# A gated attention and convolution kernel: the loading of x, the score bound and the share of VectorE in the exponentials are changed

## The chip, the cores and the metric

The kernel runs on one core of a Trainium2 chip. The core has a matrix engine (TensorE, PE in the profile), a vector engine (VectorE, DVE), an activation engine (ScalarE, ACT), a general engine (GpSimd, POOL) and a queue engine (SyncE, SP), all of which run at the same time and wait for each other through semaphores. The metric is the device time of one execution in microseconds (us), the median of several runs. TensorE writes to PSUM, a memory of eight banks of 128 x 512 float32; everything else lies in SBUF, which has 128 partitions.

## What is computed

Two branches are computed from the same x (2048 tokens x 640 features, bf16) and mixed by a gate, one number for each token. The first is a long convolution; the second is attention with 32 heads of size 20 that share one key and one value head.

```python
def reference(A_q, A_k, A_v, A_shift_k, A_ssm_k, A_ssm_D, B_x, B_wq, B_wk, B_wv, B_wo, gate_w):
    def _A_ref(q, k, v, shift_k, ssm_k, ssm_D):       # a convolution, by FFT
        ...                                           # k shifted by 4 taps, kv = k_shift * v
        y = y + kv * ssm_D[None, None, :]
        return q * y
    def _B_ref(x, wq, wk, wv, wo):
        H, Dh = 32, 20
        q = (x @ wq).reshape(B, S, H, Dh) ...
        k = x @ wk                                    # one key head for all 32 query heads
        v = x @ wv
        scores = jnp.einsum("bhqd,bkd->bhqk", q, k) * (Dh ** -0.5)
        p = _softmax(scores, axis=-1)
        o = jnp.einsum("bhqk,bkd->bhqd", p, v)
        return o ... @ wo
    x = A_q
    g = _sigmoid((x * gate_w).sum(-1, keepdims=True))
    return g * _A_ref(x, ...) + (1 - g) * _B_ref(x, ...)
```

The softmax needs 32 x 2048 x 2048 exponentials. The kernel doesn't subtract the true maximum of a row from the scores but an upper bound of it, the length of the query times the length of the longest key, in front of a fixed offset of 256 (`UP`).

## The kernel before

A small scheduler in Python, with an estimate of the duration of each operation, fixes at build time the order of the instructions on each engine. On the chip each engine then works through its list strictly in that order: an instruction that waits holds back all that stand behind it. A smaller `prio` goes first among what the scheduler thinks is ready.

**The stream of exponentials.** There are 32 groups G (four query blocks of 512 tokens x eight groups of four heads). Each has 16 key chunks j and four heads r, so there are 32 x 16 x 4 = 2048 score tiles of 128 keys x 512 queries. ScalarE takes them in turns of three tiles (`ETA`) and two tiles (`ETB`). `DVE_J[G]` lists the chunks j of a group from which two of the four tiles (a pair) go to VectorE instead.

```python
DVE_J = [()] * 5 + [(3, 8, 13)] * 27          # 27 groups x 3 = 81 pairs
...
def EXP(n):                                   # ScalarE, lines 1091
    op("act", lambda e: e.activation(et(n)[:, 0:w], self.ps[:, lo:lo + w], ACT.Exp, scale=SCALE), ...)

def DEXP(G, j):                               # VectorE: one pair, five instructions
    for h, r in enumerate(rs):                # two tiles, from PSUM to dW (line 1120)
        ... e.tensor_scalar(W[:, 512 * h:512 * h + 512], self.bank(bk), SCALE * LOG2E * 128.0, ...)
    V(lambda e: e.scalar_tensor_tensor(X[:, :], w, DP, w, ALU.add, ALU.mult), ...)            # 1123
    V(lambda e: e.scalar_tensor_tensor(X[:, :], X[:, :], DQ, w, ALU.add, ALU.mult), ...)      # 1124
    V(lambda e: e.scalar_tensor_tensor(T["ETd"]..., X[:, :], DA, W[:, :], ALU.mult, ALU.add)) # 1126
```

The products of a pair with the values come last in their group (`late_pv`): if VectorE is late with a pair, TensorE, and then ScalarE, waits at the end of the group.

**The prologue.** x is needed transposed (`xT`, features on partitions), in four blocks of 512 tokens. Three blocks come through transposing DMAs on SP's queue, the last one (block 3) is loaded plainly into `xn` and transposed by TensorE.

```python
def loads(self):
    ...                                       # wk, wv, gate_w, then 200 KB of wq on ScalarE's queue
    self.dma(T["wqst"][:, :, 0:160], wq[:, :, 0:160], ..., eng="act", prio=-98.6)
    self.dma(T["xn"][:, 12:16, :], x[:, 12:16, :], writes=[("xn", 3)], nbytes=655360, prio=-9)
    for b in range(NB - 1):                   # NB = 4
        xl = self.g.add("sp", lambda e, o=o, i=i: e.dma_start_transpose(o, i), (), [("xT", b)], 0.1, kind="d",
                        nbytes=655360, prio=-8 + b, lat=1.6)          # line 755
        xl.iss = 3.3
    ...
def tables(self):     # four rounds: VectorE makes the arguments, ScalarE the sine and the cosine
    ...               # and at last an Exp of one element, which draws in the table of Exp (line 831)
def kproj(self):
    for b in range(NB):                       # keys, replicated for four heads: group "kT", line 926
        ...
        self.evac(gr, "dve", None, ["mcol"], [("kT4", b)], ...)       # + mcol: -1 in row 20
    for b in range(NB):                       # keys, values, gate of each token: group "kvn", line 940
        ...
        self.evac(gr, "act", ... e.activation(T["ksq"]..., view(bk, 0), ACT.Square) ...)
        ...                                   # vaug, gsum; ksum: sum of the squares
    ...     # kmcol: maximum per partition; a matmul spreads it; kmaxr: maximum; kroot: its root; kmaxr: scaled
def qproj(self, I, gs, prio, banks, ng):      # queries: group "qp", line 982
    ...     # qT from PSUM; sq = qT * qT; matmul with IndG sums the squares of each head (line 998)
    self.evac(gr, "dve", ... ci[0:n, :], self.bank(bk)..., 0.5, float(0x1FBD1DF5), ALU.mult, ALU.add ...)   # root
    self.dve(lambda e: e.tensor_scalar(cr[0:n, :], ci[0:n, :].bitcast(F32), T["kmaxr"][0:n, 0:1], -UP,
                                       ALU.mult, ALU.add), [..., "kmaxr"], ["cr"], ...)                     # bound
    o = self.dma(qt[20:128:32, gs[0]:gs[0] + ng, :], cr[0:n, :], ..., name="crow")    # into row 20 of each head
    if I == 0 and gs[0] == 0:
        self.crow0 = [o]                      # much other work of the start is held back until this one
```

A score tile is then one matmul of `kT4` with `qT` over 32 rows: 20 of the head, and row 20, which subtracts the bound.

## Time and profile before

The time is 893.52 us, the median of 3 runs (893.17 to 894.32). The profiled execution has a span of 891.6 us.

| engine | busy us | share of the span | instructions |
|---|---|---|---|
| ScalarE | 868.3 | 97% | 779 |
| TensorE, matmuls | 855.1 | 96% | 7801 |
| VectorE | 658.2 | 74% | 867 |
| GpSimd | 365.6 | 41% | 311 |

The busy times count each instruction from its start to its end, and neighbours on one engine overlap a little, so the sum of the durations of a group of instructions can be above its share of the span. TensorE's list contains matmuls on zeros (916 of them at line 1511), which are only there to keep it going where it has nothing to do. The lines of the profile on which the prediction rests are shown there.

### The profile page before, as it was taken

To read this page: it belongs to the slowest core of one execution; us is meant where nothing else is said; L and a number is where in the kernel's file an instruction comes from. 1 tells how busy PE (TensorE), PEld (TensorE's weight loads), DVE (VectorE), ACT (ScalarE), POOL (GpSimd) and SP (SyncE) were. 2 spreads that over 40 slices of the span, in tenths; PEclk is the share of its full clock that TensorE was granted. 3 is DMA by queue.
4 is the path that set the end of the run, shared out by engine and by line. 5 is a ranking of instruction groups with operands and counts; after the bars stand their busy time and mean duration, and the time that the engine had idled before them with its cause. 6 is when DMAs were issued, how large, how long until landed. Compare 5 with 4: busy or idle time off the path is not lost.

```text
span 891.6 us, 17952 instructions
## 1 busy us (share of the span) xinstructions
PE 855.1 (96%) x7801; PEld 348.9 (39%) x7825; DVE 658.2 (74%) x867; ACT 868.3 (97%) x779; POOL 365.6 (41%) x311
## 2 busy tenths in 40 slices
PE   7899999999999999999999999999999999999997
PEld 3334434433433344433333334443444443343233
DVE  6457653298778788877879877768887678878674
ACT  5899999999999999999999999999999999999995
POOL 2950057860333377244427324268512677300000
PEclk9999999999999999999999999999999999999999
DMA  7930200010000011000001010000000000300211
GB/s 158 210 128 11 67 20 15 19 31 19 21 13 20 12 28 31 20 20 14 18 10 42 20 48 23 19 9 19 19 20 19 14 14 2 101 22 29 65 43 53
DMA packets 58371, 32.62 MB, mean 37 GB/s; under 512 B 41139, under 2 KB 54324, under 8 KB 58292
## 3 DMA queue, kind: packets, MB, share of 16 engines
q1 hardware_dynamic: 56026, 30.89, 12.5%
q8 instruction: 61, 1.00, 0.5%
q10 hardware_dynamic: 2266, 0.59, 0.3%
q14 instruction: 18, 0.15, 0.1%
HBM read 17.85 MB, written 6.02 MB: 27 GB/s over the span
## 4 chain that ended last, share of the span: by engine, by line
ACT 79%; PE 17%; DMA 2%; SPq 1%; DVE 1%; issue 0%; DVEq 0%
ACT ETA L1091 47%; ACT ETB L1091 32%; PE ps L1368 5%; PE ps L1059 5%; PE ps L1131 3%; PE ps L1310 1%; PE ps L982 1%; DMA kTr<-in_A_k_dram 1%; DMA xT<-in_A_q_dram 1%; SPq L755 1%; PE ps L1434 0%; SPq L1293 0%; PE ps L1511 0%; PE ps L1249 0%; DVE ETd L1126 0%
## 5 line engine op out<-in xcount | busy, mean ns | idle before, releaser
L1091 ACT ACTIVATE ETA<-ps 128x1536 bf16<-128x1536 f32 x378 | 593.4, 1570 | 3.9 <-PE ps L1059 3.4
L1091 ACT ACTIVATE ETB<-ps 128x1024 bf16<-128x1024 f32 x377 | 433.9, 1151 | 0.1
L1401 POOL TENSOR_TENSOR Pp<-X,K 128x512 f32<-128x512 bf16 x120 | 180.2, 1528 | 373.7 <-DVE K L1389 373.6
L1059 PE MATMUL ps<-qT,kT 32*128 32x512 bf16 x2048 | 300.2, 385 | 20.4 <-ACT ETA L1091 13.1
L1059 PEld LDWEIGHTS ps<-qT,kT 32*128 32x128 bf16 x2048 | 73.8, 91 | 255.4 <-ACT ETB L1091 121.7
L1131 PE MATMUL ps<-ETA,vaug 128*32 128x512 bf16 x1132 | 152.7, 385 | 0.0
L1120 DVE TENSOR_SCALAR dW<-ps 128x512 f32<-128x512 f32 x162 | 111.3, 687 | 50.7 <-PE ps L1059 49.4
L1131 PE MATMUL ps<-ETB,vaug 128*32 128x512 bf16 x754 | 148.5, 385 | 0.1
L1126 DVE SCALAR_TENSOR_TENSOR ETd<-dX,dW 128x1024 int16<-128x1024 f32 x81 | 110.6, 1366 | 25.3 <-PE ps L1131 25.0
L1123 DVE SCALAR_TENSOR_TENSOR dX<-dW 128x1024 f32<-128x1024 uint16 x81 | 111.7, 1380 | 0.9
L1124 DVE SCALAR_TENSOR_TENSOR dX<-dX,dW 128x1024 f32<-128x1024 f32 x81 | 108.7, 1341 | 0.5
L1401 POOL TENSOR_TENSOR AB<-Pp 128x256 bf16<-128x256 f32 x80 | 82.1, 1026 | 6.0
L1434 PE MATMUL ps<-AB,Tcos 128*128 128x256 bf16 x320 | 77.3, 275 | 0.0
L1511 PE MATMUL ps<-Tcos,zeros 128*32 128x512 bf16 x916 | 75.8, 385 | 0.3
L1434 PE MATMUL ps<-AB,Tsin 128*128 128x256 bf16 x280 | 68.6, 274 | 0.0
L1401 POOL TENSOR_TENSOR Pp<-Pp 128x512 f32<-128x512 f32 x40 | 61.0, 1524 | 3.1
L1368 PE MATMUL ps<-ssm_kT,Tcos 128*128 128x256 bf16 x320 | 55.3, 276 | 0.0
L1368 PE MATMUL ps<-kv,Tcos 128*128 128x256 bf16 x320 | 50.2, 275 | 0.1
L1368 PE MATMUL ps<-ssm_kT,Tsin 128*128 128x256 bf16 x320 | 49.1, 274 | 0.0
L1368 PE MATMUL ps<-kv,Tsin 128*128 128x256 bf16 x320 | 48.4, 274 | 0.0
L1131 PEld LDWEIGHTS ps<-ETA,vaug 128*32 128x32 bf16 x1132 | 29.3, 94 | 34.9 <-issue 34.0
L982 PE MATMUL ps<-xT,wq_pad 128*128 128x512 bf16 x137 | 38.9, 382 | 2.5 <-issue 1.3
(137 smaller groups left out, 746.8 us busy)
## 6 DMA issues: line engine op xcount, KB each, us to landing
rbc<-scr_d SPq DMA_DIRECT2D x31, 256.0 KB
scr_o<-oTn SPq DMA_DIRECT2D x24, 128.0 KB, 1.7
xn<-in_A_q_dram SPq DMA_DIRECT2D x4, 640.0 KB
kv<-in_A_v_dram SPq DMA_DIRECT2D x4, 640.0 KB, 4.8
out_dram<-outsb SPq DMA_DIRECT2D x14, 160.0 KB, 1.8
oTp<-scr_o SPq DMA_DIRECT2D x12, 160.0 KB, 2.8
wog<-in_B_wo_dram SPq DMA_DIRECT2D x4, 200.0 KB
wo<-in_B_wo_dram SPq DMA_DIRECT2D x4, 200.0 KB
```

Source lines behind the costliest of these rows:

```text
L982: o = self.mm(gr, lambda e, bk, gi=gi, dc=dc: e.matmul(self.bank(bk), T["wq_pad"][:, dc, 128 * gi:128 * gi + 128], T["xT"][:, dc, 512 * I: ...
L1059: return e.matmul(self.bank(bk), T["kT4"][32 * r:32 * r + 32, 128 * j:128 * j + 128], T[f"qT{G // 8 % 2}"][32 * r:32 * r + 32, G % 8, :], ...
L1091: op("act", lambda e: e.activation(et(n)[:, 0:w], self.ps[:, lo:lo + w], ACT.Exp, scale=SCALE), [("ps", base[n % 2] + k) for k in range(le ...
L1120: self.evac(gr, "dve", lambda e, bk, h=h: e.tensor_scalar(W[:, 512 * h:512 * h + 512], self.bank(bk), SCALE * LOG2E * 128.0, 128.0 * (127 ...
L1123: V(lambda e: e.scalar_tensor_tensor(X[:, :], w, DP, w, ALU.add, ALU.mult), [kW], ["dX"], c_ps(1024), **k)
L1124: V(lambda e: e.scalar_tensor_tensor(X[:, :], X[:, :], DQ, w, ALU.add, ALU.mult), [kW], ["dX"], c_ps(1024), **k)
L1126: V(lambda e: e.scalar_tensor_tensor(T["ETd"][:, :].bitcast(dt.int16), X[:, :], DA, W[:, :], ALU.mult, ALU.add), [kW, "dX"], ["ETd"], c_ps ...
L1131: return op("pe", lambda e: e.matmul(self.bank(6)[32 * r:32 * r + 32, :], T[va][:, j, :], src, start=(j == 0), stop=(j == NSC - 1), tile_p ...
L1368: self.mm(gr, lambda e, bk, lhs=lhs, rhs=rhs, comp=comp, n=n: e.matmul(self.bank(bk, 256, 256 * comp), lhs, rhs, start=(n == 0), stop=(n = ...
L1401: f = lambda e: e.tensor_tensor(out, a, b, alu)
L1434: self.mm(gr, lambda e, bk, lhs=lhs, fc=fc, comp=comp, h=h: e.matmul(self.bank(bk, 256, 256 * h), lhs, AB[:, fc, :, comp, :], start=(fc == ...
L1511: sch.filler = [[lambda e, r=r, st=st: e.matmul(self.bank(6)[32 * r:32 * r + 32, :], self.T["zeros"][:, 0:32], self.T["Tcos"][:, 0, 0:512] ...
```

## The change

The change does two things.

It hands more score tiles to VectorE: `DVE_J` names 89 pairs instead of 81. Groups 2, 3 and 4, which had none, get one each; five later groups get four instead of three; in many others the chunks move.

And it rebuilds the prologue. Half of x (blocks 2 and 3) is loaded plainly and transposed by TensorE, so that only two transposing DMAs are left; the second plain load goes out on ScalarE's queue, in the place of the first part of wq, which moves to the head of SP's queue. The bound is split: the length of the query stands in row 20 of the query and meets the length of the longest key (negative) in row 20 of the key; the offset 256 stands in row 21 of the query (`qup`) and meets a one in row 21 of the key (`q21`). So the row of the query no longer waits for the keys, and it is written in one instruction, the root as the upper 16 bits of a float, where it took two. The keys now wait for the maximum instead: `mcol` is made from it. The products "kvn" go ahead of the queries and keys, and the squares of the keys now have to come ahead of the loading of the table of Exp. Tables and constants that are not needed for the first scores get a later place.

```diff
-DVE_J = [()] * 5 + [(3, 8, 13)] * 27
+DVE_J = [(), (), (4,), (6,), (5,), (4, 9, 11), (3, 8, 13), (3, 8, 13), (3, 8, 13), (3, 9, 13), (3, 8, 13), (3, 8, 13), (2, 7, 12), (2, 6, 12), (3, 8, 14), (1, 6, 11), (3, 8, 13), (1, 8, 13), (1, 8, 12), (1, 6, 11), (1, 5, 9, 13), (3, 8, 13), (1, 4, 8, 14), (1, 6, 11), (3, 8, 12), (4, 7, 12), (2, 6, 10, 14), (2, 6, 10, 14), (1, 6, 11), (2, 6, 10, 12), (2, 9, 12), (3, 8, 13)]
 ... loads
-        self.dma(T["wqst"][:, :, 0:160], wq[:, :, 0:160], writes=[("wqst", 0)], nbytes=204800, eng="act", prio=-98.6)
+        self.dma(T["wqst"][:, :, 0:160], wq[:, :, 0:160], writes=[("wqst", 0)], nbytes=204800, prio=-10, lat=3.8)
-        self.dma(T["xn"][:, 12:16, :], x[:, 12:16, :], writes=[("xn", 3)], nbytes=655360, prio=-9)
-        for b in range(NB - 1):
+        self.dma(T["xn"][:, 12:16, :], x[:, 12:16, :], writes=[("xn", 3)], nbytes=655360, prio=-9, lat=3.8)
+        self.dma(T["xn"][:, 8:12, :], x[:, 8:12, :], writes=[("xn", 2)], nbytes=655360, eng="act", prio=-98.65, lat=3.8)
+        for b in range(NB - 2):
 ...
-                            nbytes=655360, prio=-8 + b, lat=1.6)
-            xl.iss = 3.3
+                            nbytes=655360, prio=-8 + b, lat=3.3)
+            xl.iss = 3.8
 ... tables
-            p, pr = c % 2, -2000.0 + c
+            p, pr = c % 2, (-2000.0 if c < 2 else -900.0) + c
 ... xT
-        b = NB - 1
-        for d0, nd in ((0, 2), (2, 2), (4, 1)):
+        for b, d0, nd in ((b, d0, nd) for b in (NB - 1, NB - 2) for d0, nd in ((0, 2), (2, 2), (4, 1))):
 ... kproj
-            gr = self.group("kT", (1.16 if b == 0 else 4.0) + 0.1 * b, banks=ALLB if b == 0 else (7, 4, 5))
+            gr = self.group("kT", (1.9 if b == 0 else 4.0) + 0.1 * b, banks=ALLB if b == 0 else (7, 4, 5))
-            gr = self.group("kvn", 1.5 + 0.1 * b, banks=ALLB)
+            gr = self.group("kvn", 0.9 + 0.01 * b, banks=ALLB)
 ...
+            self.sins[-1].deps.add(q)         # q: the squares; sins[-1]: the first Exp, with its table
 ...
-        self.dve(lambda e: e.tensor_scalar(T["kmaxr"][0:32, :], T["kroot"][0:32, :].bitcast(F32),
-                                           1.045 * 1.045 * 1.015, None, ALU.mult), ["kroot"], ["kmaxr"], ...)
+        self.dve(lambda e: e.scalar_tensor_tensor(T["mcol"][:, :], T["kroot"][:, :].bitcast(F32), T["m20"][:, 0:1],
+                                                  T["q21"][:, :], ALU.mult, ALU.add), ["kroot", "m20", "q21"],
+                 ["mcol"], 0.2, prio=-5000, name="kmax")
 ... qproj
-            self.evac(gr, "dve", None, (), [("qT", par, gi)], 0.7,
-                      alts=self.copy_alts(qt[:, gi, :], lambda bk: self.bank(bk)))
+            self.evac(gr, "dve", None, ["qup"], [("qT", par, gi)], 0.7, alts={...})     # + qup
 ...
-            ci[0:n, :], self.bank(bk)[0:n, :].bitcast(I32), 0.5, float(0x1FBD1DF5), ALU.mult, ALU.add), (), ...
-        self.dve(lambda e: e.tensor_scalar(cr[0:n, :], ci[0:n, :].bitcast(F32), T["kmaxr"][0:n, 0:1], -UP,
-                                           ALU.mult, ALU.add), ["ci", ("sq", 0), ("sq", 1), "kmaxr"], ["cr"], ...)
+            cr[0:n, :].bitcast(dt.int16), self.bank(bk)[0:n, :].bitcast(I32), 0.5 / 65536.0,
+            float(0x1FBD1DF5) / 65536.0, ALU.mult, ALU.add), (), ["cr"], c_ps(512), prio=pr)
 ... build
-            self.qproj(0, [2 * b, 2 * b + 1], 1.15 if b == 0 else 9.0 + 6 * b, ALLB if b == 0 else (7,), 2)
+            self.qproj(0, [2 * b, 2 * b + 1], 0.95 if b == 0 else 9.0 + 6 * b, ALLB if b == 0 else (7,), 2)
```

## The prediction

> **What bounds it now.** I read the page first for the share of each engine, then ScalarE's waits, then the chain of the first 24 us, ScalarE in the last microseconds, and the prologue on VectorE. The page:
>
> ```profile
> PE 855.1 (96%) x7801; PEld 348.9 (39%) x7825; DVE 658.2 (74%) x867; ACT 868.3 (97%) x779; POOL 365.6 (41%) x311
> ...
> ACT 79%; PE 17%; DMA 2%; SPq 1%; DVE 1%; issue 0%; DVEq 0%
> ```
>
> ScalarE and TensorE both look full, but 79% of the chain that ended last is ScalarE. All the waits of ScalarE after 24 us are one line:
>
> ```profile
> ACT ETA L1091 <- PE ps L1059: 3.4, 3, 2.3
> ```
>
> Three waits, 3.4 us together, all before 40.6 us. From there to the last exponential the stream never stops. Its ends, from the timeline:
>
> ```profile
> 40.56 1.45 ACT L1091 ACTIVATE ETA<-ps 128x1536 bf16<-128x1536 f32 x1 [0.31 <-PE ps L1059]
> ...
> 881.28 0.78 ACT L1091 ACTIVATE ETA<-ps 128x512 bf16<-128x512 f32 x1
> ```
>
> So the kernel has three parts: a prologue up to the first exponential at 23.98 us, a stream bound by ScalarE, and a tail from 882.07 us (end of the last one in the chain) to 891.6 us. The price of a tile: by the timeline six ETA and six ETB, 30 tiles, start before 40.56, and ScalarE does 2048 - 2 x 81 = 1886 in all. 1856 tiles in 841.5 us, less 0.3 for one small gate instruction, are 0.453 us each.
>
> The prologue, in the chain in order of time:
>
> ```profile
> 1.25 4.87 SPq L755
> 6.12 0.05 issue
> 6.17 6.21 DMA xT<-in_A_q_dram
> 12.38 0.04 issue
> 12.43 0.68 PE ps L940 x20
> 13.10 0.06 issue
> 13.16 2.10 PE ps L982 x9
> 15.26 1.08 PE ps L926 x5
> 16.34 0.22 PE ps L940 x9
> 16.56 0.67 ACT kT L933
> 17.23 0.02 issue
> 17.25 1.28 ACT L831
> ...
> 20.94 0.45 DVE cr L1007
> 21.39 0.03 DVE IndG L797
> 21.42 1.84 DMA qT<-cr
> ```
>
> Read three things in it. TensorE stands until 12.4 us in front of the second transposing DMA, although the first had come (the "kvn" of its block ran at 9.80); the third landed at 14.8, where SP went on. The table of Exp (L831, 1.28 us) stands in front of the last squares of the keys. And the row of the query (`cr`, then 1.84 us of DMA) waits for the maximum of the keys.
>
> [...] the trace has the 1.28 us, but the next instruction follows at once (18.54)[...]. [...] between 6 and 9 us the DMA share is already above 1, at 265 GB/s, so the second plain load will take its time from the transposes beside it. [...] `ci` from PSUM takes 0.67 us in the prologue, `cr` from SBUF 0.47, so the one instruction that is left costs what the first of the two cost. [...] the three long steps of a pair have a median of 1.22 us but means of 1.34 to 1.38 and a longest of 2.17[...].
>
> **Part 1, eight more pairs.** 2 x 8 = 16 tiles leave ScalarE: 16 x 0.453 = 7.25 us, all of it on the path, since the stream has no holes. VectorE gets 8 x (2 x 0.687 + 1.380 + 1.341 + 1.366) = 8 x 5.46 = 43.7 us, and loses about 4 us of `cr` (six at 0.67), so it is busy for some 698 us, 79% of the shorter span. On average that fits beside the stream. Locally: a group with four pairs has 64 - 8 = 56 tiles on ScalarE, 25.4 us, and in these VectorE has 4 x 5.46 = 21.8 us of pairs and about 1.8 us of normalization (0.69 + 0.25 + 0.90), before any work of the convolution. Between 570 and 810 us, where the five such groups (20, 22, 26, 27, 29) lie, VectorE was busy for 186.5 of 240 us already. Pairs have priority over the convolution, so the backlog falls on work that has time; but lists are fixed, and where one is late the end of a group stops ScalarE. Groups 2 to 4 lie at about 85 to 172 us, where VectorE is half idle (33.1 of 71 us from 100 to 171). For both I put down 0.8 us of new waits.
>
> **Part 2, the prologue.** The load: before, 1.97 MB of transposes and some 0.96 MB plain; after, 1.31 and 1.6 MB: the same 2.9 MB. The trace shows plain loads at about 358 GB/s (3.1 to 4.6 us) and transposes alone at about 290 (6.5 to 8.6). That is 1.31/0.29 + 1.6/0.358 = 9.0 us against 9.5, so the bytes alone bring little: the last block of x should land at about 13.2 us instead of 14.8. The gain lies in what follows.
>
> Path A, keys: landing 13.2; 20 small matmuls 0.68; squares 0.3; their sum 0.3; maximum per partition 0.2; spreading matmul 0.25; maximum 0.3; root and `mcol` 0.3; keys from PSUM 0.7; first scores 0.5. Together 3.5 us, so 16.7. The step from `kmcol` to scaled maximum took 19.79 to 20.88 before, which is the same size. Path B, query row: first transposed block at about 10 (behind two plain loads now), two queries 2.1 (13.16 to 15.26 before), copy 0.7, squares 0.4, matmul 0.6, root 0.67, DMA 1.84, scores 0.5: 16.8. Path C, the table: behind the last squares (14.2), 1.28 + 0.2, so 15.7: just hidden. Path D is plain work. ScalarE, from 4.4 us (its first table has come by then): eight sines and cosines at 0.62, half of six copies of transposed x (1.0, 1.0, 0.6 for each of two blocks, 2.6), a query 0.6, squares 1.0, table 1.5, keys 0.7: 11.4, so 15.8 without a hole. VectorE: 16 table steps of together 8.6, copies of x 2.0, indicators and columns 2, squares and maxima 1.9, queries and root 2.2: 16.7 from 0.8, so 17.5. TensorE does 40 transposes at 0.1 from 6.8 and about 6 us of products, so it is free enough.
>
> Four paths thus end between 15.8 and 17.5, and lists in fixed order never interlock without a hole; I take 0.5 us over the longest, 18.0 us. That is 6.0 us less than 23.98. What comes after the row of the query (loads of k and v, the rest of wq, tables) is tied to it and moves with it, so I leave the wait of 2.3 us at 37.7, for the transposed k, as it is. But the keys of blocks 1 to 3, done so far while ScalarE waited, now fall into the start of the stream: 0.1 to 0.3 us.
>
> **Sum.** 893.5 - 7.25 - 6.0 + 0.8 + 0.2 = 881.2 us.
>
> **Rivals.** (1) VectorE becomes the bound in the groups with four pairs and the new waits eat the first part. For it: 23.6 of 25.4 us there. Against it: the pairs don't have to follow the chunks in time (scores of any chunk are at hand), neighbours with three pairs leave room, and VectorE waited 49 us for scores of pairs and 25 us at `ETd`, which is slack. It would make 886 to 889. (2) The prologue gains little, because the two plain loads push the first transposing DMA back and VectorE's 17 us of work take the place of the DMA wait. For it: path D. Against it: the tables of the later rounds are out of the way of the squares now. First exponential at 20.5, total 883.7. (3) Everything overlaps and the wait for transposed k gets shorter too, since k starts to load before the stream does: first exponential at 16.5 and 2 us of the wait gone: 877.5. (4) The tail grows because the delayed work of the convolution reaches past the last exponential. VectorE was busy for 49.6 of 70 us from 810 to 880, so I give this little; it would cost 1 to 2 us.
>
> **Range and chances.** The first part is nearly fixed; its waits can spread over 0 to 4 us. The prologue can spread from -7.5 to -3.5. I say 877.5 to 886.0 for 8 in 10. Faster by 2% would need less than 875.6, which both parts at their best hardly reach: 0.03. Slower by 2% would need a stream that stops in many groups: 0.01. Within 2%: 0.96.
>
> **What would show it.** ScalarE's ETA and ETB together do 1870 tiles, with means near 1.57 and 1.15 us; the chain gives 2.26 us for each pair of them. The first ETA starts between 16.3 and 20.5 us. ScalarE's waits after its first exponential sum up to less than 6 us; VectorE is busy for about 698 us. In the chain of the prologue no table load stands in front of a square, and `cr` goes out without waiting for the keys. I am wrong if waits at the ends of groups (scores or products with VectorE's tiles) add up to over 5 us, or if the first exponential starts after 21 us, or if the tail is longer than 10.5 us.

## The result and the profile after

The changed kernel takes 886.86 us, the median of 4 runs (885.91 to 887.47), against 893.92 us of the kernel before, taken beside it. The ratio is 0.9918 with a 95% interval of 0.9901 to 0.9935. That is 7 us gained where the prediction had 12, and 0.9 us above the end of its range.

The page of the changed kernel: busy time of each engine, and the shares in the chain that ended last.

```profile
PE 851.3 (96%) x7736; PEld 347.1 (39%) x7736; DVE 685.2 (77%) x901; ACT 862.2 (97%) x773; POOL 377.3 (43%) x311
...
ACT 83%; PE 12%; DMA 2%; SPq 1%; DVE 1%; issue 0%; DVEq 0%
```

The kernel is still bound by ScalarE's stream. What the stream waits for, by the list of waits (total us, times, longest):

```profile
ACT ETA L1105 <- PE ps L1073: 5.1, 6, 2.5
```

The stream itself, from the timeline of ScalarE (start, duration, and in brackets the wait ahead of it):

```profile
23.24 1.45 ACT L1105 ACTIVATE ETA<-ps 128x1536 bf16<-128x1536 f32 x1
...
37.11 1.45 ACT L1105 ACTIVATE ETA<-ps 128x1536 bf16<-128x1536 f32 x1 [2.46 <-PE ps L1073]
...
41.21 1.45 ACT L1105 ACTIVATE ETA<-ps 128x1536 bf16<-128x1536 f32 x1 [1.49 <-PE ps L1073]
...
43.95 1.45 ACT L1105 ACTIVATE ETA<-ps 128x1536 bf16<-128x1536 f32 x1 [0.32 <-PE ps L1073]
...
235.92 1.45 ACT L1105 ACTIVATE ETA<-ps 128x1536 bf16<-128x1536 f32 x1 [0.50 <-PE ps L1073]
...
874.97 1.25 ACT L1105 ACTIVATE ETB<-ps 128x1024 bf16<-128x1024 f32 x1
```

Two things are to be seen. The first exponential comes at 23.24 us, only 0.7 earlier than before. And the start of the stream has two holes, 2.46 and 1.49 us, where it had one of 2.3. After 44 us ScalarE waits only three times, 0.16, 0.17 and 0.50 us, the last at 235.92 us; the kernel before had no wait there.

For all runs the span can be split in the same way: the first exponential, the score tiles on ScalarE at 0.4527 us each, what the stream takes beyond that, and the tail behind the last exponential. The price of a tile is that of `k_as_it_lands` below, whose stream has no wait at all: 847.51 us for 1872 tiles. (So the rest of that kernel is nought by the way it is counted; that it has no wait is measured.)

| kernel | first exponential | tiles | tiles x 0.4527 | rest of the stream | tail | span |
|---|---|---|---|---|---|---|
| before | 23.98 | 1886 | 853.8 | 4.3 | 9.5 | 891.6 |
| predicted | 18.0 | 1870 | 846.6 | 5.3 | 9.5 | 879.3 |
| changed | 23.24 | 1870 | 846.6 | 6.4 | 9.4 | 885.6 |

(The row "predicted" is the prediction's own sum: 858.1 us of stream before, less 7.25, plus 0.8 and 0.2.) The eight pairs have brought what they should. Of the 6.3 us between the two last rows, 5.2 lie ahead of the first exponential and 1.1 in the rest of the stream.

These are places in the span, though, and not yet causes. The eighth ETA, ahead of which 35 tiles are done in both kernels, starts at 43.95 us in the changed kernel. In the kernel before:

```profile
42.83 1.45 ACT L1091 ACTIVATE ETA<-ps 128x1536 bf16<-128x1536 f32 x1
```

The 0.7 us gained at the first exponential have become a loss of 1.1. What lies between is seen in the chain that ended last. In the changed kernel:

```profile
16.73 1.86 DMA qT<-cr
...
27.98 7.52 DMA kTr<-in_A_k_dram
```

and in the kernel before, behind its `21.42 1.84 DMA qT<-cr`:

```profile
27.70 7.96 DMA kTr<-in_A_k_dram
```

In both kernels this chain runs from the row of the query over the loads of the transposed k to TensorE and the next exponential, and not over the first exponential. The row went out 4.7 us earlier (16.73 instead of 21.42). But TensorE's list now waits there for the third block of k, where it waited for the second, and the two landed at nearly the same time, 35.50 and 35.66 us. So a first exponential at 18.0 us would have met this wait too. If the row had landed 2.3 us earlier, as predicted, the block would have come at some 33.2 us and the sixth ETA, which starts 1.6 us after it, at some 34.8; this is an estimate from the times above. The prediction had the sixth ETA at 37.71 - 6.0 = 31.7 us.

Why does the first exponential come so late? The first transposed block of x has landed at 10.87 us, in the chain:

```profile
1.80 9.07 DMA xT<-in_A_q_dram
```

The second transposed block of x had landed at 13.05 us (SP goes on at 13.07), as predicted (13.2). The row of the query no longer waits for the keys, also as predicted. But from 10.9 us on TensorE runs almost without a pause, 12.01 us of the 12.33 up to the first exponential. What it does with the time, from its timeline:

```profile
13.59 1.28 PE L905 MATMUL ps<-ident,xn 128*128 128x128 bf16 x20
...
15.33 1.18 PE L941 MATMUL ps<-wkv,xT 128*128 128x41 bf16 x40
16.35 1.24 PE L933 MATMUL ps<-xT,wk 128*128 128x512 bf16 x5
17.43 0.67 PE L941 MATMUL ps<-wkv,xT 128*128 128x41 bf16 x20
...
18.64 1.25 PE L992 MATMUL ps<-xT,wq_pad 128*128 128x512 bf16 x5
19.73 0.22 PE L961 MATMUL ps<-ident,kmcol 128*128 128x128 bf16 x1
```

The last "kvn" (L941, 17.43) is the start of the prediction's path of the keys. It begins 4.4 us after its block has landed, behind the transposes of the plainly loaded block 2 (whose data came at 10.3, but which stand behind the queries in the list), other "kvn", and keys. Then `kmcol` is done at 19.0, but the small matmul that spreads it (L961) has to wait for a query of block 1 (L992, 18.64), which nothing needs yet. That query is also copied by VectorE ahead of the maximum. And then the offset of the keys:

```profile
21.10 0.87 DVE L972 SCALAR_TENSOR_TENSOR mcol<-kroot,m,q 128x1 f32<-128x1 f32 x1
21.11 0.85 POOL L894 COPY wq_pad<-wqst 128x800 bf16<-128x800 bf16 x1
```

One number per partition takes 0.87 us, as long as the copy that GpSimd makes beside it (`offset_one_input` below tests this). From the landing to the first exponential it is 10.2 us; the prediction's path A had 3.5 and its half microsecond of holes.

### The profile page after: what moved, and what is told of

Its sections match the earlier page's. It is cut to its first block, busy times and chain, and to the rows that moved or that the text cites. A ratio compares the mean times of both kernels' runs of the same rounds, so it can differ in the third digit from the quotient of the medians.

```text
span 885.6 us, 17829 instructions
## 1 busy us (share of the span) xinstructions
PE 851.3 (96%) x7736; PEld 347.1 (39%) x7736; DVE 685.2 (77%) x901; ACT 862.2 (97%) x773; POOL 377.3 (43%) x311
## 4 chain that ended last, share of the span: by engine, by line
ACT 83%; PE 12%; DMA 2%; SPq 1%; DVE 1%; issue 0%; DVEq 0%
ACT ETA L1105 50%; ACT ETB L1105 34%; PE ps L1382 5%; PE ps L1073 3%; PE ps L1145 2%; DMA xT<-in_A_q_dram 1%; SPq L1307 1%; DMA kTr<-in_A_k_dram 1%; PE ps L992 1%; PE ps L1324 0%; SPq L597 0%; PE ps L1263 0%; DVE ETd L1140 0%; PE ps L1014 0%; PE ps L1386 0%; DVE dX L1137 0%
## 5 line engine op out<-in xcount | busy, mean ns | idle before, releaser
L1073 PE MATMUL ps<-qT,kT 32*128 32x512 bf16 x2048 | 297.5, 385 | 22.5 <-ACT ETA L1105 13.0
L1073 PEld LDWEIGHTS ps<-qT,kT 32*128 32x128 bf16 x2048 | 73.5, 91 | 259.3 <-ACT ETB L1105 121.7
L1134 DVE TENSOR_SCALAR dW<-ps 128x512 f32<-128x512 f32 x178 | 122.3, 687 | 47.2 <-PE ps L1073 45.5
L1140 DVE SCALAR_TENSOR_TENSOR ETd<-dX,dW 128x1024 int16<-128x1024 f32 x89 | 123.7, 1389 | 24.1 <-PE ps L1145 23.7
L1137 DVE SCALAR_TENSOR_TENSOR dX<-dW 128x1024 f32<-128x1024 uint16 x89 | 118.9, 1336 | 0.4
L1138 DVE SCALAR_TENSOR_TENSOR dX<-dX,dW 128x1024 f32<-128x1024 f32 x89 | 116.7, 1311 | 0.4
L1415 POOL TENSOR_TENSOR AB<-Pp 128x256 bf16<-128x256 f32 x80 | 90.7, 1134 | 6.0
L1525 PE MATMUL ps<-Tcos,zeros 128*32 128x512 bf16 x808 | 67.7, 384 | 0.1
L1415 POOL TENSOR_TENSOR Pp<-Pp 128x512 f32<-128x512 f32 x40 | 64.5, 1613 | 3.1
L992 PE MATMUL ps<-xT,wq_pad 128*128 128x512 bf16 x160 | 46.9, 389 | 0.7 <-DMA xT<-in_A_q_dram 0.6
```

The source lines that it names most:

```text
L992: o = self.mm(gr, lambda e, bk, gi=gi, dc=dc: e.matmul(self.bank(bk), T["wq_pad"][:, dc, 128 * gi:128 * gi + 128], T["xT"][:, dc, 512 * I: ...
L1073: return e.matmul(self.bank(bk), T["kT4"][32 * r:32 * r + 32, 128 * j:128 * j + 128], T[f"qT{G // 8 % 2}"][32 * r:32 * r + 32, G % 8, :], ...
L1134: self.evac(gr, "dve", lambda e, bk, h=h: e.tensor_scalar(W[:, 512 * h:512 * h + 512], self.bank(bk), SCALE * LOG2E * 128.0, 128.0 * (127 ...
L1140: V(lambda e: e.scalar_tensor_tensor(T["ETd"][:, :].bitcast(dt.int16), X[:, :], DA, W[:, :], ALU.mult, ALU.add), [kW, "dX"], ["ETd"], c_ps ...
L1415: f = lambda e: e.tensor_tensor(out, a, b, alu)
L1525: sch.filler = [[lambda e, r=r, st=st: e.matmul(self.bank(6)[32 * r:32 * r + 32, :], self.T["zeros"][:, 0:32], self.T["Tcos"][:, 0, 0:512] ...
```

## The experiments

Theory 1: what the prologue lacks is the order of its lists. Theory 2: the holes at 37 and 41 us come from TensorE's list, which expects the transposed k too early. Rivals: the loads (plain loads push the transposing DMAs back), engines that are full, and a stream that gives any gain back later.

### The two parts alone

The first question was whether the two parts add up, or whether the places of the pairs have to fit the rest of the lists (in the texts below, A is the theory that the pairs alone bring the whole gain, and B that their places must fit). The kernel before with the change's pairs (`pairs_same`), the same with places sought for it (`pairs_placed`), and the change with the pairs of before (`prologue_only`).

```diff
 pairs_same: before
-DVE_J = [()] * 5 + [(3, 8, 13)] * 27
+DVE_J = [(), (), (4,), (6,), (5,), (4, 9, 11), ... the list of the change
 pairs_placed: before
+DVE_J = [(), (), (4,), (7,), (4,), (6, 11), (2, 8, 11), (4, 6, 7, 13), ... also 89 pairs
 prologue_only: the change
+DVE_J = [()] * 5 + [(3, 8, 13)] * 27
```

Expected of `pairs_same`: 

> The kernel before with only the list of 89 pairs of the change. Theory A (the pairs alone bring the whole gain, wherever they stand): last exponential 7.2 us earlier at about 874.9, tail as before, 886.5 us. Theory B (the pairs only pay if their places fit the rest of the lists, because the work of the convolution must still end ahead of the last exponential): the last exponential is 7 us earlier too, but TensorE and VectorE have convolution and output products left behind it, the tail grows from 9.5 us to 20 us or more, and the time is 897 us or above.

Expected of `pairs_placed`: 

> The kernel before with 89 pairs, spread over the groups almost as in the change, but with chunks chosen so that in the lists the convolution ends in time. Theory A and B both: first exponential at 24.0 us as before, stream 7.2 us shorter, time 886 to 887 us, which is the time of the whole change. If instead the rebuilt prologue is worth something, this is slower than the whole change by that much (rival: 888 or more).

Expected of `prologue_only`: 

> The whole change, but with the 81 pairs of before. Theory A (prologue worth nothing): the first exponential at 23.2 us, but the stream 1 us behind the one of before at its 35th tile, so 894 to 895 us, and up to 3 us more if the end of the convolution no longer fits. Rival (the prologue saves something that the pairs eat up again): below 892 us.

| kernel | time | ratio to before (interval) | first exponential | rest | tail | span |
|---|---|---|---|---|---|---|
| `pairs_same` | 908.01 | 1.0156 (1.0133 to 1.0178) | 26.33 | 3.6 | 29.4 | 905.9 |
| `pairs_placed` | 891.75 | 0.9974 (0.9958 to 0.9990) | 24.62 | 7.5 | 11.2 | 889.8 |
| `prologue_only` | 898.26 | 1.0055 (1.0035 to 1.0074) | 26.72 | 4.9 | 12.8 | 898.2 |

With the same pairs, the kernel before becomes slower by 1.6%, although its stream ends at 876.5 us. The chain of `pairs_same` after that:

```profile
892.55 0.87 PE ps L1463 x5
...
893.45 0.56 DVE outsb L1466
```

The output products of the convolution branch (L1463, L1466) go one by one, 1.5 us each, up to 897 us, with nothing left to hide behind. The places of the pairs decide when VectorE and TensorE are free for the convolution, and those of the change don't fit the lists of before. This is the prediction's rival 4, which I had given little. Nor do the two parts add up: alone, the pairs are worth 2.4 us at places of their own, the prologue costs 4.1 with the old places, together they bring 7. By the expectations the first speaks for a prologue that is worth something (above 888 us), the second for one that is worth nothing or less (894 to 898 us). Neither value is the worth of a part alone: the rest of 7.5 us in `pairs_placed` and the tail of 12.8 us in `prologue_only` show places that fit less well than those of the change. The loads came up to 2 us later in these three runs than in the profiles above (third transposed block of `pairs_same` at 15.7 against 14.8, second one of `prologue_only` at 15.0 against 13.05), so in what follows the prologue is measured from the landing.

### The offset of the keys

```diff
-        self.dve(lambda e: e.scalar_tensor_tensor(T["mcol"][:, :], T["kroot"]..., T["m20"][:, 0:1], T["q21"][:, :], ...
+        self.dve(lambda e: e.tensor_scalar(T["mcol"][:, :], T["kroot"]..., T["m20"][:, 0:1], T["q21"][:, 0:1], ...
```

Expected: 

> The change with one instruction in another form: the offset of the keys (mcol) is computed with two columns as scalars instead of with a second tensor; all lists are otherwise the same. Theory: the 0.87 us that it takes are a wait for GpSimd, which copies wq at that moment (21.11 to 21.96); it falls to 0.15 us, the first exponential to 22.5 us and the time by 0.7 us. Rival (the instruction itself is slow, or the wait is for something else): it stays at 0.8 us or more, and so does the first exponential at 23.2 us.

From the timeline of `offset_one_input`, the same two instructions:

```profile
24.32 0.27 DVE L972 TENSOR_SCALAR mcol<-kroot,m,q 128x1 f32<-128x1 f32 x1
24.32 0.85 POOL L894 COPY wq_pad<-wqst 128x800 bf16<-128x800 bf16 x1
```

0.27 us instead of 0.87, beside the same copy. In `hold_block1`, below, the two-input form met a filling of `wq_pad` (18.75 to 20.45 us) and took 0.22. So the form with two tensors was long beside the copy and not beside the filling; why was not shown. But the gain expected at the first exponential is not seen. It came at 26.18 us and not at 22.5, and 11.3 us after the landing (14.88) instead of 10.2; in this profile TensorE stood for 2.94 us in front of the first transposed block, and behind that the last four matmuls of a query took 1.91 us (from 14.83), where `change_again` has 1.02; in `k_as_it_lands` below, where they took 1.91 too, the clock read 0.50 from 13.3 to 15 us. Behind that the step is comparable: from the spreading matmul (L961) to the first exponential it took 3.23 us, and 3.50 in the profiles of the change (22.95 to 26.18, 19.73 to 23.24). So 0.3 of the 0.6 us arrive; the products of the keys on TensorE, up to 25.75 us, end no earlier. The time was 888.21 us, ratio 0.9937 (0.9920 to 0.9954), which doesn't differ from that of the change.

### The query of block 1

```diff
-                    if I == 0 and gs[0]:
+                    if (I == 0 and gs[0]) or I == 1:
                         o.deps.add(self.g.writer["mcol"])
```

Expected: 

> The change, but the queries of block 1 may not start before the offset of the keys is there. Theory (things without hurry stand ahead of the maximum of the keys in TensorE's and VectorE's lists): the spreading matmul follows kmcol within 0.3 us instead of 0.85, the maximum follows it within 0.3 instead of 0.9, and from the last sum of squares (start of kmcol) to the first scores it takes 2.4 us or less instead of 3.9; the first exponential is 1.0 to 1.4 us earlier for the same loads. Rival (the path runs over the table of Exp on ScalarE, or over the row of the query): the first exponential stays. The total isn't compared, because the end of the convolution moves with every change of the lists.

Beside it ran the change again, `change_again`: 

> The change itself once more, on the chip of the three runs below, so that they have a profile of it with the same loads beside them. The loads of x came 2 us later in some runs than in others (first transposed block at 10.9 us in the first profile of the change, at 12.7 and 12.9 in later runs of the same prologue), so the first exponential is expected between 23.2 and 26.5 us, and 10.2 to 11.5 us after the last transposed block.

The change took 888.79 us (ratio 0.9941, 0.9890 to 0.9993), with the first exponential at 23.93 us, 10.2 after the landing at 13.69. In `hold_block1` the first exponential came at 22.25 us, 9.0 after the landing (13.21). Its timeline, VectorE:

```profile
19.02 0.16 DVE L958 TENSOR_REDUCE kmcol<-ksum 128x1 bf16<-128x16 f32 x1
...
20.02 0.22 DVE L972 SCALAR_TENSOR_TENSOR mcol<-kroot,m,q 128x1 f32<-128x1 f32 x1
```

From `kmcol` to the offset it is 1.0 us, where `change_again` has 2.2 (19.56 to 21.80), and to the first scores 2.5 instead of 3.9. So this part of theory 1 is shown: 1.2 us at the first exponential, some 0.3 of it perhaps from the offset, which took 0.22 us here. Its time, 915.25 us, one value, says nothing of the prologue: the tail was 37 us, since the places of the pairs no longer fitted. The same holds for the two runs that follow.

### The loads of before

The change with the loads of the kernel before: one plain block, three transposing DMAs. The first part of wq is back on ScalarE's queue, and the scheduler expects a transposed block later (`lat=4.5`), so the lists differ too.

```diff
-        self.dma(T["xn"][:, 8:12, :], x[:, 8:12, :], ..., eng="act", prio=-98.65, lat=3.8)
-        for b in range(NB - 2):
+        for b in range(NB - 1):
 ...
-        for b, d0, nd in ((b, d0, nd) for b in (NB - 1, NB - 2) for d0, nd in ((0, 2), (2, 2), (4, 1))):
+        for b, d0, nd in ((b, d0, nd) for b in (NB - 1,) for d0, nd in ((0, 2), (2, 2), (4, 1))):
```

Expected: 

> The change, but with the loads of x as before: three transposing DMAs and one block for TensorE, wq on ScalarE's queue (only the scheduler's estimate of when a transposed block arrives is later, as measured). The split bound and the order of the squares stay. Theory (what the split bound saves, the new loads lose, because the first transposed block now comes behind two plain loads and TensorE has 20 transposes more after it): the first exponential at 21 to 22.5 us, 1.5 to 4 us ahead of the change on this chip. Rival (the loads help and the split bound costs, since the keys now wait for the maximum): 24 us or later.

Measured: 915.39 us, one value (tail 38.6 us, see above), the third transposed block at 16.07 us, 2.4 later than the last one of `change_again`, but the first exponential at 21.47, 2.5 us earlier. That is 5.4 us after the landing. And even there something stood in the way, from the timeline of SP and TensorE:

```profile
17.01 0.69 SPq L597 DMA_DIRECT2D qT<-cr  x1
...
20.93 0.39 PE L1072 MATMUL ps<-qT,kT 32*128 32x512 bf16 x3 [0.19 <-DMA qT<-cr]
```

The 8 KB of the query's row, issued at 17.01 and landed at 20.8, took 3.8 us behind 600 KB of `wq` issued at 16.09; in the changed kernel they take 1.86, and 1.85 in `loads_of_before_placed` below, where this part of `wq` goes behind the row. So the split bound works without the new loads; as these came, with this order of the lists, they lost what it saves.

### The lists in the order of arrival

The new loads are kept. The copies of a transposed block don't wait for each other (each had been entered as a writer of the whole block), block 2 is expected earlier, so that its transposes come ahead of the first queries, and these ahead of "kvn", the query of block 1 behind the offset, the offset has one tensor input, and the plan is told when the loads really come.

```diff
-            self.evac(gr, "dve", None, (), [("xT", b)], 0.45, alts=al)
+            self.evac(gr, "dve", None, (), [("xT", b, d0)], 0.45, alts=al)
 ... (readers accordingly)
-    ..., eng="act", prio=-98.65, lat=3.8)
+    ..., eng="act", prio=-98.65, lat=1.5)
-    nbytes=655360, prio=-8 + b, lat=3.3)
+    nbytes=655360, prio=-8 + b, lat=4.3 if b == 0 else 3.3)
-            self.qproj(0, [2 * b, 2 * b + 1], 0.95 if b == 0 else 9.0 + 6 * b, ...
+            self.qproj(0, [2 * b, 2 * b + 1], 0.85 if b == 0 else 9.0 + 6 * b, ...
 ... and the edits of offset_one_input and hold_block1
```

Expected: 

> The change with the new loads, but with lists in the order in which data come: the three copies of one transposed block don't wait for each other, the second block for TensorE is taken as arriving before the first transposing DMA, the first queries ahead of the keys' products, queries of block 1 after the offset, the offset with one input. Theory (order of the lists, not the loads and not the sum of the work, makes the prologue slow): first exponential 2 to 3.5 us ahead of the change on this chip. Rival 1 (loads: the first transposed block sets it): within 0.7 us of the change. Rival 2 (ScalarE and VectorE are simply full until then): within 0.7 us too, with both at over 90% from 9 us to the first exponential. The end of the convolution is expected to lie beyond the last exponential here, so the total isn't compared.

Measured: 912.68 us, one value, with a tail of 37.6 us. The first exponential came at 21.00 us, 7.6 after the landing (13.41), with the same loads: 2.9 us before that of `change_again`, and the eleventh ETA is 5 us ahead of it (44.85 against 49.81). The order of the lists, with the offset's instruction in it, brings 2.6 us from the landing on. With the same loads and the same engines, that can't be put down to the loads, nor to a VectorE that was full.

### With places that fit

For these lists I sought new places for the pairs, with the scheduler's plan, until the planned end of the convolution lay as close behind the last exponential as in the change; this left 87 or 88 pairs. `in_order_placed` and `in_order_88` also know how long the loads of k and v take:

```diff
-                           nbytes=655360, prio=14 + b, lat=1.6, after=self.crow0, name="ld_k")
-            x.iss = 3.3
+                           nbytes=655360, prio=14 + b, lat=2.4, after=self.crow0, name="ld_k")
+            x.iss = 4.7
-                     prio=14.5 + b, name="ld_v", after=self.crow0)
+                     prio=14.5 + b, name="ld_v", after=self.crow0, lat=4.0)
```

`loads_of_before_placed` has these estimates too, with the loads of before, the rest of `wq` behind the query's row, and the edits above that apply to it.

Expected of `change_third`: 

> The change as it is, to have it on the same chip as the three kernels sent with it. 886 to 889 us; first exponential 10.2 us after the second transposed block of x has landed (23.2 to 24 us); the sixth and seventh ETA wait 1.7 to 2.5 and 1.0 to 1.5 us for scores.

Expected of `in_order_placed`: 

> The change with its lists in the order of arrival (as in lists_in_order), with the loads of k and v estimated as long as they take, and with places for 87 pairs sought so that the planned end of the convolution lies as near the last exponential as in the change. Theory (what the prologue lacked was the order of the lists, not loads or full engines, and the early waits are for k coming later than the plan has it): first exponential 7.6 to 8 us after the landing instead of 10.2 (about 21 us), -2.6; the two waits at 37 to 42 us fall from 3.5 to below 1.5, -2; two pairs fewer, +1.8; tail 9 to 10 us: in all 2.5 to 3 us less than the change, 883 to 886. Rival (the stream takes any gain back, because it can't run ahead of k and the convolution): the same as the change or longer, with waits or a tail grown by 3 us.

Expected of `in_order_88`: 

> The same kernel with other places, for 88 pairs, with a planned end 0.4 us later. Theory: within 1.5 us of in_order_placed, one pair more in the stream (-0.9), tail 0.5 to 1.5 longer. If the places make more than 3 us of difference, the tail or waits at ends of groups show it, and the plan's end says little of the time.

Expected of `loads_of_before_placed`: 

> The change's split bound and order of the keys, with the loads of the kernel before (one plain block of x, three transposing DMAs, the first part of wq on ScalarE's queue), the rest of wq behind the query row, copies of transposed blocks that don't wait for each other, the offset in an instruction with one tensor, k and v as long as they take, and places sought for 87 pairs. Theory (the new loads lose what the split bound saves): first exponential at 20.5 to 21.5 us against 23.2 to 24 for the change, -2.5; the query row's DMA 1.9 us instead of 3.8; early waits below 1.5, -2; two pairs fewer +1.8; tail 9 to 10: 883 to 886, level with in_order_placed. Rival (the new loads are worth their 2 us once the lists fit): 2 us slower than in_order_placed.

All four on one chip:

| kernel | time | ratio to before (interval) | first exponential (after landing) | rest | tail | span |
|---|---|---|---|---|---|---|
| `change_third` | 887.51 | 0.9933 (0.9919 to 0.9946) | 24.37 (10.2) | 5.5 | 9.4 | 885.8 |
| `in_order_placed` | 882.92 | 0.9879 (0.9865 to 0.9892) | 21.48 (7.5) | 1.8 | 9.4 | 881.1 |
| `in_order_88` | 883.61 | 0.9897 (0.9878 to 0.9916) | 21.51 (7.5) | 1.9 | 11.0 | 881.8 |
| `loads_of_before_placed` | 882.19 | 0.9872 (0.9858 to 0.9885) | 20.70 (5.3) | 1.9 | 9.5 | 880.5 |

The two with 87 pairs are a little faster than the 883 to 886 us expected. Theory 1 holds for the first exponential: in the order of arrival it comes 2.7 us earlier from the landing on. `in_order_placed` is also 4.6 us faster than the change, with two pairs fewer, but it has the estimates for k and v as well: 2.9 us of the difference lie ahead of the first exponential and 3.7 in the rest of the stream, and the two pairs cost 1.8. What the order is worth in time is taken up in the next part. The loads of before are level with the new ones (the intervals overlap), so half of x through TensorE is worth nothing that these runs can show. What may limit the prologue of `in_order_placed`, from the timeline of TensorE, and below it the whole stretch up to the first exponential (length, then the busy us of TensorE, its weight loads, VectorE, ScalarE and GpSimd, then granted clock, share of DMA and GB/s):

```profile
11.28 1.29 PE L905 MATMUL ps<-ident,xn 128*128 128x128 bf16 x20 [0.62 <-DMA xn<-in_A_q_dram]
```

```profile
11.28:21.48 10.20, 9.78 (x131) 5.74 (x133) 8.96 (x31) 7.22 (x14) 1.32 (x1) 1.00 0.52 123
```

From the arrival of the second plain block on, TensorE is busy for 9.78 of 10.2 us, VectorE for 8.96. So it is TensorE that has least room there; that it sets the time is argued, since no run takes work off it and leaves all else. With the loads of before it has its work earlier and runs matmuls on zeros (L1533) in between.

### The holes alone

```diff
 the change, with the three lines for k and v above, and places for 88 pairs; nothing else
```

Expected: 

> The change with nothing but the estimates for the loads of k and v set to what the trace shows, and places for 88 pairs sought to go with it; the prologue's lists stay as they are. Theory (the waits at 37 and 41 us come from TensorE's list, which puts products of the transposed k ahead of scores before k is there; TensorE then stands 2 us and runs at half the granted clock for some us after): first exponential still 10 us after the second transposed block (23 to 25 us), no wait of TensorE on k above 0.7 us, granted clock 1.0 from 36 to 44 us, ScalarE's waits in the stream 4 to 5 us down to below 2; 1 pair fewer costs 0.9; so 884.5 to 887, 1.5 to 2.5 us less than the change on the same ground. Rival (the holes are only a sign that the stream can't run ahead of its work there): waits of 2 us or more come up elsewhere before 60 us.

Measured: 882.63 us (882.29 to 883.69), ratio 0.9864 (0.9843 to 0.9886); first exponential at 24.98 us, 11.6 after the landing (13.38), rest 0.1 us, tail 9.4, span 881.9. The waits are gone, all of them, which is more than I expected, and the eighth ETA starts at 40.63 us, 3.3 us before that of the change, although the first exponential came later. So most of what the change missed in time is won back at k, with no gain at the first exponential (the places of the pairs, which differ too, may have a share). The order of the prologue adds nothing to this that the times show: `in_order_88`, with as many pairs, has its first exponential 3.5 us earlier, but 1.8 us more of rest and 1.6 more of tail, and takes 883.61 us, and the intervals of all these kernels overlap. The rival that the stream gives back what the prologue gains is thus not refuted.

How the waits arise is seen in the changed kernel, TensorE's timeline:

```profile
35.54 0.93 PE L1324 MATMUL ps<-kdiag,kTr 128*128 128x128 bf16 x7 [2.10 <-DMA kTr<-in_A_k_dram]
36.40 0.61 PE L1073 MATMUL ps<-qT,kT 32*128 32x512 bf16 x3
```

The shifted products of k (L1324) stand in the list ahead of the scores (L1073) that ScalarE waits for, and k is not there. A stall of 2.10 us makes the hole of 2.46. The second hole has no stall ahead of it, but a slow clock. Stretches of the changed kernel, in the columns named above:

```profile
35.50:37.20 1.70, 1.66 (x13) 1.03 (x14) 0.00 (x0) 0.09 (x1) 1.70 (x4) 0.50 0.91 323
37.20:42.10 4.90, 4.90 (x28) 1.32 (x25) 0.69 (x1) 3.27 (x3) 4.90 (x9) 0.50 1.07 237
```

Behind the stall TensorE has a clock of 0.50 for 6.8 us, from 35.5 to 42.3 us. That this makes the second hole is seen by comparison with `offset_one_input`, which has the same lists. There the stall was 2.29 us, but the clock stayed at 1.00 (TensorE's timeline, the stretch after the stall, ScalarE's timeline):

```profile
39.10 0.56 PE L1324 MATMUL ps<-kdiag,kTr 128*128 128x128 bf16 x7 [2.29 <-DMA kTr<-in_A_k_dram]
...
39.10:42.40 3.30, 3.14 (x34) 1.53 (x36) 0.37 (x1) 2.31 (x2) 3.30 (x7) 1.00 1.10 283
...
42.43 1.45 ACT L1105 ACTIVATE ETA<-ps 128x1536 bf16<-128x1536 f32 x1
```

The sixth ETA waits for 2.29 us, the seventh (42.43) not at all. In the three profiles of the change, with a clock of 0.50 there (in the two repeats from 38 to 40 us), the seventh waits for 1.49, 1.05 and 0.89 us. No run set the clock by itself, so this is a comparison and no test. Nor is the clock of 1.00 all gain: in `offset_one_input` the eighth ETA (46.25) waits for 1.46 us. A stretch of `k_as_it_lands` in the same place:

```profile
36.00:38.00 2.00, 1.85 (x26) 0.95 (x25) 0.37 (x2) 2.00 (x3) 2.00 (x5) 1.00 0.92 196
```

The clock stays at 1.00 and ScalarE is busy throughout, up to 44 us. In the stretches above the clock is 1.00 or 0.50. It fell to 0.50 at the end of a stall of 2.10 us, and in the kernel before at the end of one of 1.75 us (0.50 from 35.55 to 38.9 us); it did not behind one of 2.29 us in `offset_one_input`, nor behind one of 1.74 us in the kernel before, up to 12.43 us (1.00 from 11.3 to 19 us). So the length of the stall alone doesn't decide; what does was not shown.

## Why the prediction was wrong

By its own steps:

- **Eight more pairs, -7.25 us: right.** The changed kernel has 1870 tiles on ScalarE. The new waits for which 0.8 us had been put down came to 0.83 us, all between 107 and 236 us. VectorE is busy for 685 us, not 698: a pair costs 5.41 us on average now, where it was 5.46; of the instructions for the bound ten went and not six; and other instructions of VectorE got a little shorter (`xn` times `gf` takes 0.380 us on average, 16 times, where it took 0.453).
- **The last block of x at 13.2 us: right** (13.05; 13.7 and 14.2 in the two repeats), **with some luck.** The prediction's sum, 9.0 us of loading against 9.5, makes it 0.5 us earlier than 14.8 and not 1.6, and in two other runs with the same loads it came at 14.9 and 15.0. The first transposed block came at 10.87, "about 10" said I.
- **Path A, 3.5 us from the landing: the step that failed for the first exponential.** It was 10.2 us. The links that I summed have the lengths that I gave them, but for the offset (0.87 instead of some 0.2). What was missing are the entries that stand between them in the same lists: 4.4 us from the landing to the last "kvn", and 1.3 us between `kmcol` and the maximum, because of a query of block 1. With the 0.7 of the offset that is 6.4 of the 6.7 us. "TensorE does 40 transposes at 0.1 from 6.8 and about 6 us of products, so it is free enough" is the sentence that went wrong: I compared its sum with the whole prologue. In the 12.33 us from 10.91 to the first exponential TensorE is busy for 12.01, VectorE only for 9.06. "0.5 us over the longest" was meant to cover the order of the lists; the order cost 2.7 us (`in_order_placed` against `change_third`, 7.5 against 10.2 from the landing, some 0.3 of it the offset's instruction). The rest up to 18.0 us would be TensorE's own work, which is argued only.
- **The wait of 2.3 us at 37.7, "tied to" the row of the query and left "as it is": the step that failed for the time.** The row went out 4.7 us earlier, and the wait did not move with it: it ended at 35.5 us, where it had ended at 35.7, because TensorE's list, made anew, had one block of k more ahead of the scores. It grew, to 2.46 and 1.49 us, and by the eighth ETA nothing was left of what the prologue had gained. It is no property of the loads but of the plan, which has k come too early. `k_as_it_lands` shows that three estimates, with places of the pairs to fit, are worth the whole rest: 4.9 us less than `change_third`, with one pair fewer and no gain at the first exponential.
- **Paths B, C and the tail: the mechanisms right.** `cr` goes out at 16.7 us without waiting for the keys, the table load stands behind the squares (18.57), the tail is 9.4 us. But each came late, for the same cause as path A: the row of the query had landed at 18.6 us instead of 16.3, behind transposes and "kvn" that came first on TensorE and VectorE, and the table load began 4.4 us later than in path C, because the last squares did.

Of the rivals, the second had the right result, a prologue that gains little, and part of the reason: the loads had a share (the first exponential came 2.5 us earlier in `old_loads` than in `change_again`, and 0.8 us earlier in `loads_of_before_placed` than in `in_order_placed`), but where it named VectorE it was the order of the lists. The first had the right time for a wrong reason: between 570 and 810 us, where the groups with four pairs lie, ScalarE never waits. The fourth didn't happen in the change, but the tail grew by 20 to 29 us in the four kernels whose lists or places were changed one without the other (`pairs_same`, `hold_block1`, `old_loads`, `lists_in_order`), and by 3.3 us in `prologue_only`.

In time, the change kept 7 of its 12 us. Three kernels, at 882.2 to 882.9 us, are faster than the change: the upper ends of their intervals (0.9885 to 0.9892) lie below the lower ends of the change in its first measurement and in `change_third` (0.9901 and 0.9919); the wide interval of `change_again` begins at 0.9890. All three have the estimates for k and v; two have the order of the lists besides, with either set of loads. What sets the landing of x stays open: the second transposed block came between 13.05 and 15.0 us with the same loads, and between 13.2 and 15.0 on one and the same chip. From the landing on, this prologue took 10.2 us in three profiles, and 11.3 to 11.7 in three others (`offset_one_input`, `k_as_it_lands`, `prologue_only`). In the last two of these the clock was 0.50 from 13.3 to 15 us; in the first, four matmuls of a query took 1.91 us, as in `k_as_it_lands`.

## What to carry to other kernels

Where engines work through fixed lists, don't size a path by the links of its own chain: write down what stands in each engine's list between the arrival of the data and the last link, and sum that. Before counting a gain at the head of a stream, see what the stream waits for next: here it was k, and the gain ended there. After a change to loads, put the measured landings into whatever orders the lists; a product placed ahead of its data costs its wait and here often a slower TensorE after it (2.10 us and 6.8 us at a clock of 0.50 in the changed kernel), both on the instructions behind it. And when one part of a kernel was tuned to fill the gaps of another, as the pairs here, test neither part alone without fitting the other to it.

## What the runs showed of the hardware

- At the end of stalls of TensorE of 1.75 us (kernel before, up to 35.72 us) and 2.10 us (changed kernel, up to 35.54 us) the granted clock fell to 0.50, until 38.9 us and 42.3 us. Behind others it was 1.00: 1.74 us in the kernel before (up to 12.43 us) and 2.29 us in `offset_one_input`. The same in the prologue, in front of the first transposed block: 0.50 from 13.3 to 15 us behind 2.19 and 3.50 us (`k_as_it_lands`, `prologue_only`), 1.00 from 11.3 to 19 us behind 2.49 us (`change_third`). Behind 2.94 us in `offset_one_input` four matmuls of a query took 1.91 us, as in `k_as_it_lands`; behind 1.85 us in `change_again` 1.02 us, as in `change_third`.
- An 8 KB DMA took 3.8 us behind 600 KB issued 0.9 us ahead of it (`old_loads`), and 1.85 us when those were issued behind it (`loads_of_before_placed`).
- A VectorE instruction on one element per partition took 0.87 us beside a GpSimd copy when it had two tensors to read (changed kernel, `change_again`), 0.27 us with one tensor beside that copy (`offset_one_input`), and 0.22 us with two beside a filling (`hold_block1`). One tensor is no guarantee: in `hold_block1` a cast of four elements per partition (`IndG`) took 0.64 us beside the same copy, and 0.17 us after it.
